# Stage a of a Fourier and maxout kernel as four 48x64 matmuls on quarters of the array, batches 3 to 7

## Chip, cores and metric

One core of one Trainium2 chip. The metric is the device time of one execution in microseconds (us). Times of the kernel before come from three runs and from one further execution that the hardware profiler recorded.

## What is computed

The input `x` has 8 batches of 3072 positions with 256 features. Each batch goes through a real Fourier transform along the positions, a complex 256x256 product with a bias, a soft threshold and the inverse transform. Every position then goes through three 256x768 products, whose elementwise maximum goes through a 768x256 product.

```
X = np.fft.rfft(x, axis=1)
Yr = Xr @ w_r - Xi @ w_i + b_r
Yi = Xr @ w_i + Xi @ w_r + b_i
Y = np.sign(Y) * np.maximum(np.abs(Y) - 0.01, 0.0)      # both parts
y = np.fft.irfft(Y, n=3072, axis=1)
h = np.maximum(np.maximum(y @ w1, y @ w2), y @ w3)
out = h @ w_out
```

## The kernel before

A position is written as n = 32*n1 + n2, with 96 values of n1 and 32 of n2. The forward transform has two steps. **Stage a** multiplies by a 96x96 table over n1: `load_x` (L460 on) brings four values of n2, a *quad*, as 96 rows of 1024 numbers (4 x 256 features); `split_x` makes two float16 halves of it, a high one on ACT and the remainder on DVE; `stage_a` multiplies the table, which is split likewise, by them and writes the result through `aq` to `a_d` in DRAM. Eight quads make a batch. **Stage b** (`load_a`, `split_a`, `stage_b`) reads `a_d` back in another layout and transforms over n2. `stage_w`, `stage_w2` and `finish_w` do the complex product and the threshold, `stage_q` begins the inverse transform and writes `z_d`, and `load_z`, `split_z` and `inverse` end it. `up` (three products and their maximum) and `down` do the rest.

A float32 product is made of three float16 ones, high by high, low by high and high by low: `mm3` issues them at L172, L173 and L174. So in stage a of batches 3 to 7 (the quads from `HALF_X` = 24 on, 40 in all) a quad is two groups of three matmuls, each with a 96x96 table as weights and 512 moving columns. The halves of that table (`f16`) lie in the tile `zeros`, whose name the profile shows. Batches 0 to 2 do stage a in float32 or in fp32r and are not touched.

The main loop runs over batches, over eight chunks of 384 positions, and over six slots (`f`) of a chunk. A slot is `up` for three weights (18 matmuls of 384 columns into three PSUM banks of the tag `up`) and `down` of an earlier slot (nine matmuls of 256 columns). All other stages of the next batch are put between the parts of the slots by a table of positions (`at`), measured in slots: a quad has position p = 5.6 slots per quad, loads at p - 8, `split_x` at p, `stage_a` at p + 1. `run_until` runs what is due, and a scheduler keeps each engine's instructions in the resulting order. The small operands come from the pools named in the code: `xq` has two buffers, the PSUM tiles `pa`, `px`, `py`, `pz` and `pi` share three banks (tag `ff`), and the tags `vl` and `vh` have three SBUF buffers each, used by batch 0 alone.

The lines that matter below: L172 to L174 (matmuls), L535 (ACT takes `pa` out of PSUM into `aq`), L539 (the ACT queue issues the store), L166 and L167 (the two halves of a split, on ACT and DVE), L905, L908 and L911 (ACT takes the first product of a slot out of PSUM, DVE the other two), L466 (load of a quad).

## Time and profile before

| | |
|---|---|
| median of 3 runs | 2024.7 us (2024.07 to 2025.35) |
| the profiled execution: its own time | 2026.48 us |
| its span, first to last instruction | 2024.7 us |
| TensorE (PE) busy | 2005.9 us, 99% |
| VectorE (DVE) busy | 1427.9 us, 71% |
| ScalarE (ACT) busy | 1046.7 us, 52% |
| granted TensorE clock | 0.999 of 2.4 GHz |

A matmul's duration in the profile counts from its start until its last result, and the next one starts earlier than that; what a matmul costs in a dense stream is the distance between two starts. PEld is the weight load, which the profile shows on a row of its own. An engine's idle time is put down to what released it.

### The profile page before, as it was taken

The page shows a single profiled execution, that of the slowest core. Times are in us where ns is not written, and L with a number is a line of the kernel's source. Part 1 is how long each engine was busy: PE and PEld are TensorE (multiplying, and loading weights), DVE is VectorE, ACT ScalarE, POOL GpSimd, SP SyncE. Part 2 cuts the span into 40 slices and gives each one's busy share as a digit, 9 for nine tenths or more (in the row PEclk, how much of TensorE's full clock was granted, in tenths as well). Part 3 has the DMA queues.
Part 4 walks back from the last instruction along what each step waited for, and adds up shares of the span by engine and source line. Part 5 has one row for each costly group of instructions (what it writes and reads, how often), then busy time and mean ns, then how long its engine had stood idle before and what let it go on. Part 6 is the DMA issues. An engine that isn't in the chain of part 4 may idle for free.

```text
span 2024.7 us, 40265 instructions
## 1 busy us (share of the span) xinstructions
PE 2005.9 (99%) x15822; PEld 1405.1 (69%) x15822; DVE 1427.9 (71%) x2726; ACT 1046.7 (52%) x2052; POOL 19.9 (1%) x75
## 2 busy tenths in 40 slices
PE   9999999999999999999999999999999999999999
PEld 5756766677776776767776777667777677776666
DVE  3787887687866877668776778757876577764454
ACT  4755654456545555455554565545554455543333
POOL 0000000000000000000000000000000000000000
PEclk9999999999999999999999999999999999999999
DMA  9645553454442453335442454333442333311110
GB/s 299 198 149 139 147 137 101 112 138 131 111 120 81 131 143 95 110 102 136 131 112 87 119 138 117 105 103 86 128 113 61 89 93 94 82 53 32 32 32 24
DMA packets 204560, 223.48 MB, mean 110 GB/s; under 512 B 20787, under 2 KB 179123, under 8 KB 204275
## 3 DMA queue, kind: packets, MB, share of 16 engines
q1 hardware_dynamic: 143603, 145.39, 27.6%
q10 hardware_dynamic: 59744, 72.11, 11.2%
q0 software_dynamic: 1024, 3.41, 0.5%
q8 instruction: 125, 2.05, 0.4%
q14 instruction: 64, 0.52, 0.1%
HBM read 103.13 MB, written 75.50 MB: 88 GB/s over the span
## 4 chain that ended last, share of the span: by engine, by line
PE 95%; DVE 2%; DMA 1%; ACT 1%; issue 1%; SPq 0%; ACTq 0%; DVEq 0%
PE pu L172 18%; PE pu L174 18%; PE pu L173 18%; PE pd L174 6%; PE pd L173 6%; PE pd L172 6%; PE py L174 3%; PE py L173 3%; PE py L172 3%; PE px L675 2%; PE pa L532 1%; PE pi L174 1%; PE pi L172 1%; PE pa L172 1%; PE pi L173 1%; PE pa L174 1%
## 5 line engine op out<-in xcount | busy, mean ns | idle before, releaser
L172 PE MATMUL pu<-yh,wuh 128*128 128x384 f16 x2304 | 751.8, 326 | 3.0 <-ACT c L905 1.0
L174 PE MATMUL pu<-yh,wul 128*128 128x384 f16 x2304 | 751.3, 326 | 0.0
L173 PE MATMUL pu<-yl,wuh 128*128 128x384 f16 x2304 | 751.3, 326 | 0.0
L166 ACT ACTIVATE hh<-h 128x384 f16<-128x384 f32 x384 | 200.3, 522 | 501.3 <-DVE h L911 497.8
L908 DVE TENSOR_TENSOR c<-pu,c 128x384 f32<-128x384 f32 x384 | 212.5, 553 | 257.5 <-PE pu L174 154.1
L174 PEld LDWEIGHTS <-wul 128*128 128x128 f16 x2304 | 225.4, 98 | 149.7 <-issue 0.7
L173 PE MATMUL pd<-wol,hh 128*128 128x256 f16 x1152 | 313.8, 273 | 0.0
L172 PE MATMUL pd<-woh,hh 128*128 128x256 f16 x1152 | 313.8, 273 | 0.0
L173 PEld LDWEIGHTS <-wuh 128*128 128x128 f16 x2304 | 225.7, 98 | 126.8 <-issue 4.9
L174 PE MATMUL pd<-woh,hh 128*128 128x256 f16 x1152 | 313.5, 273 | 0.0
L172 PEld LDWEIGHTS <-wuh 128*128 128x128 f16 x2304 | 225.5, 98 | 124.4 <-issue 3.2
L167 DVE SCALAR_TENSOR_TENSOR hh<-h,hh 128x384 f16<-128x384 f32 x384 | 213.5, 556 | 135.0 <-ACT hh L166 132.9
L905 ACT ACTIVATE c<-pu 128x384 f32<-128x384 f32 x384 | 187.0, 487 | 175.9 <-PE pu L174 155.1
L911 DVE TENSOR_TENSOR h<-pu,c 128x384 f32<-128x384 f32 x384 | 211.7, 551 | 50.2 <-PE pu L174 46.4
L172 PE MATMUL py<-wch,tt 128*128 128x256 f16 x504 | 137.4, 273 | 0.0
L174 PE MATMUL py<-wch,tt 128*128 128x256 f16 x504 | 137.3, 273 | 0.0
L173 PE MATMUL py<-wcl,tt 128*128 128x256 f16 x504 | 137.3, 272 | 0.0
L172 PEld LDWEIGHTS <-hh 128*128 128x128 f16 x1152 | 112.7, 98 | 33.7 <-issue 0.3
L173 PEld LDWEIGHTS <-hh 128*128 128x128 f16 x1152 | 112.7, 98 | 33.4
L940 ACT ACTIVATE o<-pd,s1u 128x256 f32<-128x256 f32 x191 | 82.8, 467 | 76.8 <-PE pd L174 35.4
L174 PEld LDWEIGHTS <-hh 128*128 128x128 f16 x1152 | 112.7, 98 | 13.8 <-DVE hh L167 0.5
L167 DVE SCALAR_TENSOR_TENSOR zl<-zq,s0u,zh 96x1024 f16<-96x1024 f32 (+1 forms) x72 | 82.7, 1157 | 4.4 <-ACT zh L166 4.3
(219 smaller groups left out, 2633.0 us busy)
## 6 DMA issues: line engine op xcount, KB each, us to landing
z_d<-zs ACTq DMA_DIRECT2D x96, 256.0 KB, 3.0
out_dram<-o ACTq DMA_DIRECT2D x190, 128.0 KB, 2.1
zq<-z_d SPq DMA_DIRECT2D x63, 384.0 KB, 4.0
ab<-a_d SPq DMA_DIRECT2D x84, 256.0 KB, 4.0
ab<-ab SPq DMA_DIRECT2D x336, 64.0 KB, 2.2
xq<-in_x_dram SPq DMA_DIRECT2D x55, 384.0 KB, 4.0
a_d<-aq ACTq DMA_DIRECT2D x53, 384.0 KB, 3.4
vb<-vb SPq DMA_DIRECT2D x308, 64.0 KB, 2.6
```

The source lines that it names most:

```text
L166: nc.scalar.activation(out=hi, in_=src, func=AF.Copy, scale=scale)
L167: later(lambda: low(nc.vector.scalar_tensor_tensor(out=lo, in0=src, scalar=scale, in1=h, op0=ALU.mult, op1=ALU.subtract)))
L172: nc.tensor.matmul(o, lh, rh, start=start, stop=False, **kw)
L173: nc.tensor.matmul(o, lh, rl, start=False, stop=False, **kw)
L174: st["mm"] = nc.tensor.matmul(o, ll, rh, start=False, stop=stop, **kw)
L532: nc.tensor.matmul(pa[0:96], fr, xp, start=True, stop=True)
L675: nc.tensor.matmul(pv[:, h, :, g // 2, g % 2], ah[:, g // 2, g % 2, h * P:(h + 1) * P], mb_sb[:, i, 4 * kb + g].rearrange("p (c m) -> p c ...
L905: st["act"] = nc.scalar.activation(out=c1, in_=p, func=AF.Copy)
L908: st["dve"] = nc.vector.tensor_tensor(out=c1, in0=p, in1=c1, op=ALU.max)
L911: st["dve"] = nc.vector.tensor_tensor(out=h32, in0=p, in1=st["c1"], op=ALU.max)
L940: nc.scalar.activation(out=o, in_=pd[t], func=AF.Copy, scale=st[b, "su"][1])
```

## The change

For n1 and n1 + 48 the table's rows are equal in the columns of even k1 and opposite in those of odd k1. So the change computes the 48 sums x[n1] + x[n1+48] and the 48 differences, and multiplies the sums by the 48 even columns and the differences by the 48 odd ones. The sums lie in partitions 0 to 47, the differences in 64 to 111. The tables are padded to 64 columns. Each product is cut into its two halves of 512 columns (`h`), and these go to PSUM partitions 0 to 63 and 64 to 127, so that four matmuls of 48 rows by 64 columns can lie on the four quarters of the array. A quad is then 12 matmuls of 512 columns, in three rounds of four, each with its own weight load, where there were six.

The operand takes four more loads and one cut in two: `xq` is loaded as rows 0 to 63 and, below them, again rows 0 to 47; a second pair of tiles (`x2`, in the buffers of `vl` and `vh`) gets the rows that lie 48 further on. A new step `sum_x`, one slot ahead of `split_x`, adds on DVE the second to the first with a sign per partition. The store becomes four.

```diff
+    even, odd = (np.pad(fa[0:48, np.arange(96) % 4 // 2 == i], ((0, 16), (0, 16))) for i in (1, 0))
+    tiled = np.block([[z, even], [z, odd]])
...
-    f16 = [zeros[0:N1, 128 * i:128 * i + 96] for i in range(2)]
+    ft = zeros[:, 384:512].rearrange("p (i m) -> p i m", i=2)
...
+    sign = small("sign")
+    nc.vector.memset(sign[0:64], 1.0)
+    nc.vector.memset(sign[64:P], -1.0)
...
-                xq = fft.tile([N1, NQ * D], F32, name="xq", bufs=2)
+                xq = fft.tile([P, NQ * D], F32, name="xq", bufs=2)
+                if q >= HALF_X:
+                    second = [
+                        fft.tile([P, 2, D], F32, name="x2", tag=tag, bufs=3) for tag in ("vl", "vh")
+                    ]
+                    xn = xq.rearrange("p (n d) -> p n d", n=NQ)
+                    for r, n in ((0, 64), (64, 48)):
+                        nc.sync.dma_start(out=xn[r:r + n], in_=xv[0:n])
+                    for i, t in enumerate(second):
+                        for r, n in ((0, 48), (48, 64)):
+                            nc.sync.dma_start(out=t[r:r + n], in_=xv[96 - n:96, 2 * i:2 * i + 2])
+                    st["x", q] = xq, second
+                    return
...
+    def sum_x(q):
+        xq, second = st.pop(("x", q))
+        with in_turn():
+            for i, t in enumerate(second):
+                half = xq[0:112, i * 512:i * 512 + 512]
+                nc.vector.scalar_tensor_tensor(
+                    out=half, in0=t[0:112].rearrange("p n d -> p (n d)"), scalar=sign[0:112], in1=half,
+                    op0=ALU.mult, op1=ALU.add,
+                )
+        st["x", q] = xq
...
     def split_x(q):
+        if q >= HALF_X:
+            xt = x_tile().bitcast(F16).rearrange("p i (h d) -> p i h d", h=2)[0:112]
+            for i in range(2):
+                with in_turn():
+                    split_later(
+                        xt[:, 0, i], xt[:, 1, i], pairs[0:112, i * 512:i * 512 + 512], st[b, "xx"][0:112]
+                    )
+            st["xs", q] = xt
+            return
...
     def stage_a(q):
+        if q >= HALF_X:
+            xt = st.pop(("xs", q))
+            pa = [ff_tile("pa") for _ in range(2)]
+            aq = fft.tile([P, NQ * D], F32, name="aq", bufs=2)
+            for t, i in ((0, 0), (0, 1), (1, 0)):
+                for r in range(2):
+                    rows = slice(64 * r, 64 * r + 48)
+                    for h in range(2):
+                        st["mm"] = nc.tensor.matmul(
+                            pa[r][64 * h:64 * h + 64], ft[rows, t], xt[rows, i, h],
+                            start=t == i, stop=t == 1,
+                        )
+            av = batch(b, "a").rearrange("(k e c) n d -> e k c (n d)", e=2, c=2)
+            for r in range(2):
+                o = aq[:, 512 * r:512 * r + 512]
+                nc.scalar.activation(out=o, in_=pa[r], func=AF.Copy, scale=1.0 / (X_SCALE * F_SCALE))
+                for h in range(2):
+                    n = q4 * NQ * D + h * 512
+                    nc.scalar.dma_start(out=av[1 - r, :, :, n:n + 512], in_=o[64 * h:64 * h + 48])
+            return
...
         at(p - (3 if b == 1 else 5 if b == 2 else 8), load_x, q)
+        if q >= HALF_X:
+            at(p - 1, sum_x, q)
         at(p, split_x, q)
         at(p + 1, stage_a, q)
```

Each engine's order shows where these stand. On PE, the last quad of batch 7 stood like this between two `up` products (`pa` is its PSUM bank, `xhl` the split operand, `zeros` the tile with the table):

```order
L174 MATMUL pu_20907<-yh_20754,wul_82 128x384
L172 LDWEIGHTS zeros_72
L172 MATMUL pa_20918<-xhl_20873,zeros_72 96x512
L173 LDWEIGHTS zeros_72
L173 MATMUL pa_20918<-xhl_20873,zeros_72 96x512
L174 LDWEIGHTS zeros_72
L174 MATMUL pa_20918<-xhl_20873,zeros_72 96x512
```

Now the same place has four matmuls, two to each of two banks, before the first bank is written again:

```order
L176 MATMUL pu_21583<-yh_21429,wul_82 128x384
L568 LDWEIGHTS zeros_72
L568 MATMUL pa_21593<-xhl_21550,zeros_72 64x512
L568 LDWEIGHTS zeros_72
L568 MATMUL pa_21593<-xhl_21550,zeros_72 64x512
L568 LDWEIGHTS zeros_72
L568 MATMUL pa_21594<-xhl_21550,zeros_72 64x512
L568 LDWEIGHTS zeros_72
L568 MATMUL pa_21594<-xhl_21550,zeros_72 64x512
L568 LDWEIGHTS zeros_72
L568 MATMUL pa_21593<-xhl_21550,zeros_72 64x512
```

Weight load and matmul still alternate, and the stage stands between the same neighbours.

On DVE, ahead of the same quad's split (`c1` and `h32` are the two results of `up` that DVE takes out of PSUM, `hh` and `yl` are remainders of splits), there stood:

```order
L911 TENSOR_TENSOR h32_20793<-pu_20786,c1_20751 128x384
L167 SCALAR_TENSOR_TENSOR hh_20795<-h32_20793,hh_20795 128x384
L167 SCALAR_TENSOR_TENSOR yl_20755<-pi_20806,yh_20754 128x384
L908 TENSOR_TENSOR c1_20827<-pu_20831,c1_20827 128x384
L911 TENSOR_TENSOR h32_20846<-pu_20839,c1_20827 128x384
L167 SCALAR_TENSOR_TENSOR hh_20848<-h32_20846,hh_20848 128x384
L908 TENSOR_TENSOR c1_20869<-pu_20877,c1_20869 128x384
L167 SCALAR_TENSOR_TENSOR xhl_20873<-xq_20336,xx_17743,xhl_20873 96x512
L167 SCALAR_TENSOR_TENSOR xhl_20875<-xq_20336,xx_17743,xhl_20875 96x512
```

and now:

```order
L965 TENSOR_TENSOR h32_21468<-pu_21461,c1_21426 128x384
L525 SCALAR_TENSOR_TENSOR xq_20994<-x2_20995,sign_91,xq_20994 112x512
L169 SCALAR_TENSOR_TENSOR hh_21470<-h32_21468,hh_21470 128x384
L525 SCALAR_TENSOR_TENSOR xq_20994<-x2_20996,sign_91,xq_20994 112x512
L169 SCALAR_TENSOR_TENSOR yl_21430<-pi_21481,yh_21429 128x384
L962 TENSOR_TENSOR c1_21502<-pu_21508,c1_21502 128x384
L965 TENSOR_TENSOR h32_21523<-pu_21516,c1_21502 128x384
L169 SCALAR_TENSOR_TENSOR hh_21525<-h32_21523,hh_21525 128x384
L962 TENSOR_TENSOR c1_21546<-pu_21553,c1_21546 128x384
L169 SCALAR_TENSOR_TENSOR xhl_21550<-xq_20994,xx_18299,xhl_21550 112x512 x2
```

The two sums come about one slot ahead of the split, with the remainder of `hh` and two PSUM results of `up` behind them.

On ACT the end of that quad was

```order
L905 ACTIVATE c1_20914<-pu_20907 128x384
L535 ACTIVATE aq_20917<-pa_20918 96x512
L535 ACTIVATE aq_20917<-pa_20923 96x512
L539 DMA a_d_18073<-aq_20917 96x1024
L820 ACTIVATE zs_20944<-pz_20937,s1v_14370 128x512
```

and is now

```order
L959 ACTIVATE c1_21590<-pu_21583 128x384
L575 ACTIVATE aq_21595<-pa_21593 128x512
L575 ACTIVATE aq_21595<-pa_21594 128x512
L578 DMA a_d_18641<-aq_21595 24x2x512 x4
L872 ACTIVATE zs_21629<-pz_21622,s1v_14790 128x512
```

Four stores stand where one stood; the rest is in the same order.

## Rows read from the trace of the kernel before

**Rows 1.** From the page: busy time of the engines, the granted clock in 40 slices (tenths), and the shares of the chain of work that ended last.

```profile
PE 2005.9 (99%) x15822; PEld 1405.1 (69%) x15822; DVE 1427.9 (71%) x2726; ACT 1046.7 (52%) x2052; POOL 19.9 (1%) x75
...
PEclk9999999999999999999999999999999999999999
...
PE 95%; DVE 2%; DMA 1%; ACT 1%; issue 1%; SPq 0%; ACTq 0%; DVEq 0%
```

**Rows 2.** Busy time by stretch; stage a of batches 3 to 7 runs from 382 to 1570 us. The columns are named in the first row.

```profile
core 0: us, PE busy (x) PEld busy (x) DVE busy (x) ACT busy (x) POOL busy (x), PEclk, DMA share, GB/s
...
380.00:680.00 300.00, 300.00 (x2468) 211.96 (x2467) 222.80 (x412) 161.83 (x321) 1.84 (x8) 1.00 0.43 116
680.00:980.00 300.00, 298.85 (x2448) 211.03 (x2446) 226.03 (x418) 161.97 (x321) 1.84 (x8) 1.00 0.44 120
980.00:1280.00 300.00, 300.00 (x2463) 212.09 (x2461) 224.78 (x416) 163.06 (x324) 1.84 (x8) 1.00 0.43 117
1280.00:1570.00 290.00, 289.63 (x2347) 204.00 (x2346) 204.58 (x386) 151.84 (x299) 3.68 (x16) 1.00 0.36 98
```

**Rows 3.** PE matmuls by line and shape over the whole run: count, busy us, mean ns of one, idle us of PE just before them and what ended it.

```profile
L172 PE MATMUL pu<-yh,wuh 128*128 128x384 f16 x2304 | 751.8, 326 | 3.0 <-ACT c L905 1.0 <-DVE c L908 1.0 <-ACT yh L166 0.4
...
L675 PE MATMUL px<-mb_all,ab 128*128 128x64 f16 x1344 | 53.0, 193 | 0.0
L172 PE MATMUL pa<-xhl,zeros 96*96 96x512 f16 x80 | 30.4, 380 | 0.0
L174 PE MATMUL pa<-xhl,zeros 96*96 96x512 f16 x80 | 30.3, 378 | 0.0
L173 PE MATMUL pa<-xhl,zeros 96*96 96x512 f16 x80 | 30.2, 378 | 0.0
L172 PE MATMUL pz<-vb,qh 128*128 128x512 f16 x77 | 29.2, 379 | 3.1 <-DMA vb<-vb 3.0
```

**Rows 4.** PE in order of time through the last quad of stage a: start us, duration us, line, operation.

```profile
1567.88 0.33 PE L174 MATMUL pu<-yh,wul 128*128 128x384 f16 x1
1568.04 0.38 PE L172 MATMUL pa<-xhl,zeros 96*96 96x512 f16 x1
1568.26 0.38 PE L173 MATMUL pa<-xhl,zeros 96*96 96x512 f16 x1
1568.47 0.38 PE L174 MATMUL pa<-xhl,zeros 96*96 96x512 f16 x1
1568.69 0.38 PE L172 MATMUL pa<-xhl,zeros 96*96 96x512 f16 x1
1568.90 0.38 PE L173 MATMUL pa<-xhl,zeros 96*96 96x512 f16 x1
1569.12 0.38 PE L174 MATMUL pa<-xhl,zeros 96*96 96x512 f16 x1
1569.34 0.33 PE L172 MATMUL pu<-yh,wuh 128*128 128x384 f16 x1
```

**Rows 5.** PE in order of time through one `stage_b`: the row of x16 is 16 matmuls of 64 columns, each with its own weight load.

```profile
1408.21 0.63 PE L675 MATMUL px<-mb_all,ab 128*128 128x64 f16 x16
1408.67 0.33 PE L172 MATMUL pu<-yh,wuh 128*128 128x384 f16 x1
```

**Rows 6.** Weight loads by line and shape over the whole run: count, busy us, mean ns of one.

```profile
L172 PEld LDWEIGHTS <-hh 128*128 128x128 f16 x1152 | 112.7, 98 | 33.7 <-issue 0.3
...
L172 PEld LDWEIGHTS <-zeros 96*96 96x96 f16 x80 | 9.8, 123 | 5.5
```

**Rows 7.** Weight loads in order of time in the last quad of stage a.

```profile
1567.88 0.12 PEld L172 LDWEIGHTS <-zeros 96*96 96x96 f16 x1
1568.04 0.12 PEld L173 LDWEIGHTS <-zeros 96*96 96x96 f16 x1
1568.26 0.12 PEld L174 LDWEIGHTS <-zeros 96*96 96x96 f16 x1
```

**Rows 8.** DVE instructions by line and shape over the whole run: count, busy us, mean ns of one, idle us before them.

```profile
L908 DVE TENSOR_TENSOR c<-pu,c 128x384 f32<-128x384 f32 x384 | 212.5, 553 | 257.5 <-PE pu L174 154.1 <-ACT c L905 96.5 <-ACT zh L166 5.0
...
L772 DVE SCALAR_TENSOR_TENSOR u<-py,s1x,cs 128x512 f32<-128x512 f32 x77 | 57.5, 747 | 25.0 <-PE py L174 20.8 <-ACT cs L762 4.2
...
L167 DVE SCALAR_TENSOR_TENSOR xhl<-xq,xx,xhl 96x512 f16<-96x512 f32 x80 | 56.8, 741 | 0.5
...
L581 DVE SCALAR_TENSOR_TENSOR ab<-ab 128x512 f16<-128x512 f32 x60 | 41.0, 683 | 4.8 <-ACT ab L578 4.0
```

**Rows 9.** DVE in order of time around the last quad: start us, duration us, line, operation, idle us before and what ended it.

```profile
1565.38 0.56 DVE L908 TENSOR_TENSOR c<-pu,c 128x384 f32<-128x384 f32 x1 [1.30 <-PE pu L174]
1565.85 1.40 DVE L167 SCALAR_TENSOR_TENSOR xhl<-xq,xx,xhl 96x512 f16<-96x512 f32 x2
1567.17 0.55 DVE L911 TENSOR_TENSOR h<-pu,c 128x384 f32<-128x384 f32 x1
1568.31 0.56 DVE L167 SCALAR_TENSOR_TENSOR hh<-h,hh 128x384 f16<-128x384 f32 x1 [0.59 <-ACT hh L166]
1570.58 0.56 DVE L908 TENSOR_TENSOR c<-pu,c 128x384 f32<-128x384 f32 x1 [1.71 <-PE pu L174]
```

**Rows 10.** ACT and its queue behind the same quad.

```profile
1568.89 1.24 ACT L535 ACTIVATE aq<-pa 96x512 f32<-96x512 f32 x2 [0.16 <-PE pa L174]
1570.16 0.33 ACTq L539 DMA_DIRECT2D a_d<-aq  x1
```

**Rows 11.** Waits of the SP queue: line, what it waited for, us in total, times, longest.

```profile
SPq L466 <- DVE xhl L167: 275.5, 25, 20.6
```

**Rows 12.** From the page: DMA issues, with count, KB each and median us from issue to landing.

```profile
xq<-in_x_dram SPq DMA_DIRECT2D x55, 384.0 KB, 4.0
a_d<-aq ACTq DMA_DIRECT2D x53, 384.0 KB, 3.4
vb<-vb SPq DMA_DIRECT2D x308, 64.0 KB, 2.6
```

More of the change, by code (lines that the diff above doesn't have):

```diff
@@ L88, in dft_tables @@
         halves(np.stack([np.concatenate([v, v]) for v in blocks], 1), SB),
-        np.ascontiguousarray(np.stack(mq + mb, 1)).astype(np.float32),
+        np.ascontiguousarray(np.stack(mq + mb + [tiled], 1)).astype(np.float32),
         np.eye(128, dtype=np.float32),
@@ L210, in quad_tile @@
     def quad_tile(name):
-        return fft.tile([96, NQ * D], F32, name=name, bufs=1 if name == "zq" else 2)
+        return fft.tile([P, NQ * D], F32, name=name, bufs=1 if name == "zq" else 2)[0:96]
     def s_tile(name):
@@ L240, in load_tables @@
         nc.sync.dma_start(out=id_sb, in_=ident)
+        st["tiled"] = s_tile("tiled")[:, 0:P]
+        nc.sync.dma_start(out=st["tiled"], in_=mq[:, 26])
     def load_last_bias():
@@ L464, in load_x @@
             else:
-                xq = fft.tile([N1, NQ * D], F32, name="xq", bufs=2)
+                xq = fft.tile([P, NQ * D], F32, name="xq", bufs=2)
[11 more added lines that the diff above has]
+                    return
+                xq = xq[0:N1]
             nc.sync.dma_start(out=xq.rearrange("p (n d) -> p n d", n=NQ), in_=xv)
@@ L502, in split_x @@
         pairs = st.pop(("x", q))
+        if q >= HALF_X:
[7 more added lines that the diff above has]
+            return
         parts = []
         for i, xp in enumerate(pairs):
-            if q >= HALF_X:
-                xt = x_tile().bitcast(F16)[0:N1]
-                xh, xl = xt[:, 0, 0:2 * D], xt[:, 1, 0:2 * D]
-                with in_turn():
-                    split_later(xh, xl, xp, st[b, "xx"][0:N1])
-                parts.append((xh, xl))
-                continue
             if q >= EARLY:
@@ L533, in stage_a @@
             else:
-                mm3(pa[0:96], *(f16 if q >= HALF_X else (fh, fl)), *xp)
+                mm3(pa[0:96], fh, fl, *xp)
             nc.scalar.activation(
-                out=aq[:, i * 512:i * 512 + 512], in_=pa[0:96], func=AF.Copy,
-                scale=1.0 / (X_SCALE * F_SCALE) if q >= HALF_X else 1.0,
+                out=aq[:, i * 512:i * 512 + 512], in_=pa[0:96], func=AF.Copy
             )
@@ L1019, in fourier_maxout_kernel @@
             if k == 0:
-                split_scaled(*f16, fr, F_SCALE)
+                split_scaled(ft[:, 0], ft[:, 1], st["tiled"][:, 64:P], F_SCALE)
             if k in (-2, 1, 4):
```

## Prediction

> **What bounds the kernel now.** I read the page first. PE is busy for 99% of the span, the chain of work that ended last lies on PE for 95%, and the granted clock is at its upper level, 2.4 GHz, in every slice [rows 1]; all prices below are at that level. Then the busy times by stretch: in the four stretches from 380 to 1570 us, where the changed stage runs, PE is idle for 1190.0 - 1188.5 = 1.5 us, while DVE is busy for 878 of 1190 us (74%) and ACT for 639 (54%) [rows 2]. So there a microsecond taken from the stream of matmuls is a microsecond of the kernel, and work on another engine costs nothing until it makes PE wait. The idle time by group says how little that happens: 3.0 us in front of 2304 matmuls of `up` and 3.1 us in front of `pz` [rows 3]. Last I read PE in order of time through one quad of stage a [rows 4].
>
> **What the change removes.** A matmul of the old stage lasts 0.38 us by its row [rows 3], but six of them start 0.216 us apart, and the next `up` starts 1569.34 - 1568.04 = 1.30 us after the first [rows 4]. That is the price in a dense stream. Forty quads (80 groups of three) hold 40 x 1.30 = 52.0 us.
>
> **What it puts there.** Twelve matmuls of 512 columns, each with a weight load. How long they take depends on how many are on the array at once, which no row of the trace before shows; I bound it. If none overlaps, a quad takes 12 x 0.216 = 2.59 us. If four overlap fully, 3 x 0.216 = 0.65 us. Between these, two smaller terms. Issue: in `stage_b` 16 pairs of weight load and matmul pass in 1408.67 - 1408.21 = 0.46 us, 0.029 us a pair [rows 5], so PE can hand out four pairs in 0.12 us, well inside the 0.216 us that one of them streams. Issue is then not the limit; it only staggers the four, and the last ends 3 x 0.029 = 0.09 us late: 0.65 + 0.09 = 0.74 us. I take the overlap as given, because the four matmuls of a round share nothing: two halves of the rows, two halves of the columns, two PSUM banks. Weight loads: one for 96 columns lasts 0.123 us against 0.098 us for 128 columns [rows 6], yet each starts with the matmul before it and is over long before that one is [rows 7], and the matmuls keep their 0.216 us. I expect the same of the 64-column ones.
>
> The second term is the passage between the whole array and its quarters, twice a quad. The lower end is nothing: from 128x128 to 96x96 weights and back PE shows ordinary distances, 0.16 and 0.22 us [rows 4]. The upper end is that each passage waits for the last results to leave, 0.38 - 0.216 = 0.163 us, and then exposes a weight load of 0.123 us: 2 x 0.286 = 0.57 us. I take one residue, 0.16 us, on the lower side of the middle, since the nearest row, the change of weight shape, costs nothing. A quad is then 0.74 + 0.16 = 0.90 us, and 40 x (1.30 - 0.90) = **16.0 us** go.
>
> The Trainium skill has a rule against this (TensorEngine Tiling (Array Packing), Tiling Modes, Key Properties): going from one tiling mode to another drains the engine. No run here shows a passage between modes. By that rule, paid in full at both ends, the sum would be about nothing instead of 16 us; it is the first rival.
>
> **What it adds elsewhere, each hidden.**
> - *DVE, two sums a quad.* The nearest rows are float32 operations of the same width, 0.683 us with a constant factor and 0.747 us with one per partition [rows 8]; I take 0.74. Eighty make 59 us, so DVE goes from 74% to 79% in that stretch. What could suffer is the release of PSUM banks. The product taken out at 1565.38 is done at 1565.94, and its bank is next written at 1569.34, three `up` products on [rows 4, 9]: 3.4 us to spare, against 1.48 us for both sums. DVE also stands idle for 154 us waiting for PE in front of L908 alone [rows 8]. If the slack were gone, the cost would be up to 40 x 1.48 = 59 us.
> - *DVE and ACT, the split.* The instructions keep their number and width (512 columns); 112 partitions instead of 96 change nothing that I charge. The sums stand a slot ahead of the split, some 5 us, and so do not delay it. The remainder of the second half is needed at the second matmul round instead of the fifth matmul; it is ready at 1567.25 and used from 1568.04 on [rows 4, 9].
> - *ACT, the store.* Four issues instead of one, 0.33 us each [rows 10]: 1 us more a quad, 40 us in all, on an engine that is half idle. Behind them stands the next `c` of `up`. Price if exposed: 40 us.
> - *PSUM.* Both `pa` banks are needed from the third matmul, 0.06 us in, not 0.65 us. There are three banks, and PE is not seen waiting for one here, so nothing is charged.
> - *SP, the loads.* Six issues of 896 KB in place of one of 384 KB: 40 x 512 KB = 20 MB more, 18 GB/s on the 98 to 120 GB/s of these stretches [rows 2]. The queue already stands still for a free `xq` for 275 us in 25 waits, up to 20.6 us each [rows 11]: loads are issued as early as a buffer allows and are needed far later than the 4.0 us that one takes to land [rows 12]. Five more issues hold the queue for perhaps 2 us a quad, an estimate from the 0.33 us of an issue on the other queue [rows 10] with some room. Behind them wait the moves of `vb`, 2.6 us to landing [rows 12], for which `pz` has waited 3.0 us in all [rows 3]. A late move could cost up to that 2 us in a few places; I charge nothing and keep it for the range.
> - *The start.* One 64 KB load and two small memsets before 50 us; nothing.
>
> **The sum.** The profiled execution took 2026.5 us, 1.8 us more than its span, which equals the median of the runs. 2026.5 - 16.0 = 2010.5 us for a profiled execution, 2008.7 us for a median run: **2009 us**. With both bounds of the switch and no other stall: 40 x (1.30 - 0.74) = 22 us less, 2002 us; with no stagger either, 26 us less, 1999 us; with 0.57 us of switching, nothing gained, 2025 us.
>
> **The rivals.**
> - *The passages eat the gain.* Each quad pays 0.34 to 0.6 us at its two ends: 1.08 to 1.34 us, so 2016 to 2026 us. For it: two passages a quad, 80 in all, for only three rounds of work between. Against it: the other changes of shape in rows 4 are free. Chance 0.17 (faster 0.07, same 0.06, slower 0.04).
> - *Slower: a weight load waits for the matmul on its own rows.* The place is inside a round. If the load for the right-hand quarter may not enter while the left-hand quarter of the same rows streams, the two column halves go one after the other and only the two row halves run side by side: six matmuls in turn per half. With the load behind the stream that is 6 x (0.216 + 0.029) = 1.47 us, 2024.7 + 40 x 0.17 = 2032 us; with the load behind the last result, 6 x (0.38 + 0.12) = 3.0 us and 2093 us. It decides from the point where a round takes over 1.30 / 3 = 0.43 us. Against it: on the whole array the load of the next weights starts with the matmul before it, on the same rows [rows 4, 7]. Chance 0.10. The Trainium skill states this rule (TensorE: Matmul & The Clock Gate, Part 3, what overlaps and what doesn't): weight loads overlap with running matmuls only where the row group differs. The trace disagrees for the whole array, at 1568.04; for quarters nothing here shows it.
> - *Nothing overlaps,* the change doesn't do what it says: 2.59 us a quad, 2024.7 + 40 x 1.29 = 2076 us. Nothing in the trace excludes it. Chance 0.06.
> - *A late engine.* The sums, the stores or the loads make PE wait. With 0.2 to 0.6 us a quad, 2017 to 2033 us; with both sums exposed, 2009 + 59 = 2068 us. Against it: the idle time of DVE and ACT in [rows 2, 9]. Chance 0.10 (faster 0.04, same 0.02, slower 0.04).
>
> **How the numbers follow.** About 0.2%, 4 us, is what a measurement can tell from no change. The forecast, quarters side by side with at most 0.34 us of switching, 1999 to 2016 us, has the rest, 0.57. Faster: 0.57 + 0.07 + 0.04 = 0.68. Same: 0.06 + 0.02 = 0.08. Slower: 0.04 + 0.10 + 0.06 + 0.04 = 0.24. The range runs from 2000 us, the full overlap, to 2035 us, past the first rival and the mild ends of the second and fourth. It leaves out the case of no overlap (0.06), most of the second rival (0.08), the far end of the fourth (0.03) and a hair below.
>
> **What would show it.** In the profile after, four starts of the new matmuls should lie within 0.1 us, rounds 0.22 us apart, and the next matmul of another kind should start about 0.90 us after the first; 0.74 means free passages, 1.3 that they eat the gain, and 1.47 or more that rounds do not hold together. DVE should be some 59 us busier with PE idle for no more than 3 us between 380 and 1570 us. The prediction is wrong in its main step if starts in a round lie 0.2 us apart, and in its cover if PE waits for DVE, ACT or a DMA there for over 5 us.

## The result, and the profile after

The change made the kernel slower: 2048.02 us, median of 4 runs (2047.35 to 2051.04), against 2025.03 us before (2024.07 to 2025.38). The ratio is 1.0117, interval 1.01 to 1.0135. The profiled execution took 2047.66 us, with a span of 2045.9 us, 21.2 us more than before. The forecast was 2009 us with a range up to 2035 us.

The first view is again the page: busy times, then the chain that ended last.

```profile
PE 2001.0 (98%) x16062; PEld 1384.5 (68%) x16062; DVE 1470.4 (72%) x2808; ACT 1036.0 (51%) x2052; POOL 22.4 (1%) x75
...
PE 48%; DVE 5%; DMA 4%; ACT 3%; issue 2%; ACTq 2%; SPq 0%; DVEq 0%
```

Beside [rows 1] the chain has changed its kind: PE's share has fallen from 95% to 48%, and the chain now runs through DVE, ACT, ACT's queue (ACTq) and transfers. (These shares add up to 64% only, where those before came near the whole span; so I read from this line which engines came onto the chain, and no sizes.) The clock is not the reason: it stands at its upper level in every slice, as before, 0.997 on average.

The second view is the busy time by stretch: from, to, length, then busy microseconds of PE, weight loads, DVE, ACT and POOL with their counts, granted clock, share of the DMA engines, GB/s.

```profile
380.00:680.00 300.00, 294.17 (x2501) 203.50 (x2500) 231.50 (x429) 155.86 (x314) 2.87 (x8) 1.00 0.48 132
680.00:980.00 300.00, 294.60 (x2499) 204.38 (x2498) 231.43 (x431) 158.61 (x321) 2.22 (x8) 1.00 0.49 135
980.00:1280.00 300.00, 291.15 (x2440) 200.51 (x2438) 229.99 (x429) 154.36 (x311) 2.21 (x8) 0.99 0.48 133
1280.00:1570.00 290.00, 281.26 (x2364) 194.39 (x2361) 211.00 (x397) 148.83 (x298) 4.43 (x16) 1.00 0.42 115
sum 1190.00, PE 1161.18 PEld 802.78 DVE 903.92 ACT 617.65 POOL 11.74; mean PE 290.29 PEld 200.70 DVE 225.98 ACT 154.41 POOL 2.93
```

PE is idle for 1190.0 - 1161.2 = 28.8 us where [rows 2] had 1.5 us. DVE is not full (904 of 1190 us), and ACT is *less* busy than before. Nothing here is an overloaded engine; something is late.

**Did the matmuls do what was forecast?** PE in order of time through the last quad of stage a, then the groups by form:

```profile
1588.96 0.33 PE L176 MATMUL pu<-yh,wul 128*128 128x384 f16 x1
1589.22 0.84 PE L568 MATMUL pa<-xhl,zeros 48*64 48x512 f16 x12
1589.99 0.34 PE L174 MATMUL pu<-yh,wuh 128*128 128x384 f16 x1
```

```profile
1589.21 0.36 PEld L568 LDWEIGHTS <-zeros 48*64 48x64 f16 x12 [0.32 <-issue]
```

```profile
L568 PE MATMUL pa<-xhl,zeros 48*64 48x512 f16 x480 | 33.7, 384 | 0.0
...
L525 DVE SCALAR_TENSOR_TENSOR xq<-x,sign,xq 112x512 f32<-112x512 f32 x80 | 57.8, 754 | 0.0
...
L174 PE MATMUL pu<-yh,wuh 128*128 128x384 f16 x2304 | 752.5, 327 | 14.2 <-ACT c L959 12.3 <-DVE c L962 1.0 <-DVE h L965 0.4
```

Yes. Twelve matmuls take 1589.99 - 1589.22 = 0.77 us where six took 1.30 us [rows 4]. Each matmul lasts 384 ns on its own, but 480 of them cover only 33.7 us: they overlap. The single records show starts at 0, 3, 6 and 10 ns, then 240 to 250 ns, then 456 to 466 ns: four at once, in three rounds. The sums cost DVE what was forecast (57.8 us) and never left it idle in front of them. What is new stands in the third row: 14.2 us of idle time in front of `up` [rows 3: 3.0 us], 12.3 us of it ended by ACT's `c`.

**Where the time went.** I take the stretch from the first matmul of the new stage to its last, and sum distances between starts of neighbouring matmuls, since busy times overlap and hide part of a wait. What a distance has above the ordinary one of its shape (0.16 us behind 384 columns, [rows 4]), if it is over 0.03 us, counts as PE waiting.

| in the stretch, us | before | after | difference |
|---|---|---|---|
| 40 quads of stage a, first start to next `up` | 51.9 | 31.0 | -20.9 |
| 40 distances ahead of the first `pa` | 5.7 | 9.4 | +3.7 |
| PE waiting elsewhere | 2.1 | 39.1 | +37.0 |
| stretch as a whole | 1186.5 | 1206.9 | +20.4 |

The three terms give +19.8 us of the +20.4. Ahead of the stretch and behind it nothing changed (382.6 and 382.8 us; 455.6 and 456.2 us). So the matmuls gave 17.2 us, and a new wait took 37.

**The new wait.** The list of waits: engine, line and what it waited for, us in total, times, longest. Then the issues of the store, as counts with shortest, median and longest duration in ns.

```profile
ACT zs L872 <- DMA a_d<-aq: 45.6, 14, 5.0
...
ACT c L959 <- DMA a_d<-aq: 29.1, 10, 3.4
ACT hh L168 <- DMA a_d<-aq: 28.8, 10, 3.5
...
PE pu L174 <- ACT c L959: 12.3, 15, 1.5
...
PE pd L174 <- ACT o L994: 4.9, 9, 0.9
```

```profile
L578 ACTq DMA_DIRECT2D a_d<-aq x160: 740/750/1517, 384.7 to 1593.2; - x160
```

ACT stands still for over 100 us under this heading, which the list of the kernel before does not have. Nearly all of it (95.6 of 103.5 us) stands right behind a store of `aq`. These are not waits for data to land: `zs` reads nothing of `aq`. The issues are made by ACT's own sequencer, and ACT's order in time shows what that means, first in an ordinary quad, then in the worst one:

```profile
1216.20 1.06 ACT L575 ACTIVATE aq<-pa 128x512 f32<-128x512 f32 x2
1216.81 3.24 ACTq L578 DMA_DIRECT2D a_d<-aq  x4
1220.10 0.69 ACT L872 ACTIVATE zs<-pz,s1v 128x512 f32<-128x512 f32 x1 [2.83 <-DMA a_d<-aq]
...
1246.61 1.06 ACT L575 ACTIVATE aq<-pa 128x512 f32<-128x512 f32 x2
1247.22 5.35 ACTq L578 DMA_DIRECT2D a_d<-aq  x4
1252.67 0.69 ACT L872 ACTIVATE zs<-pz,s1v 128x512 f32<-128x512 f32 x1 [5.00 <-DMA a_d<-aq]
1253.26 0.51 ACT L168 ACTIVATE hh<-h 128x384 f16<-128x384 f32 x1
...
1253.80 0.49 ACT L959 ACTIVATE c<-pu 128x384 f32<-128x384 f32 x1
...
1254.35 0.32 PE L174 MATMUL pu<-yh,wuh 128*128 128x384 f16 x1 [1.45 <-ACT c L959]
```

Four issues follow each other for 3.24 us, and ACT begins nothing else meanwhile. An issue takes 0.75 us, not the 0.33 us of [rows 10]. Behind them stand `zs`, `hh` and `c`, and PE stands 1.45 us at 1254.35 for the bank that `c` takes out. At 1247 even more came together: the chain of waits shows the third issue held until a store of the output had landed.

```profile
1244.44 6.53 DMA out_dram<-o
1250.97 0.02 issue
1250.99 0.02 ACTq L578
1251.01 0.04 issue
1251.05 0.74 ACTq L578
```

In 9 of the 40 quads the four issues took over 3.5 us. In five of these an issue began late, behind a wait like this one, in four a single issue itself lasted 1.1 to 1.5 us. All quads together took 9.0 us above 3.25 us a quad.

### The profile page after: what moved, and what is told of

It is laid out like the page before. It is cut to its first block, busy times and chain, and to the rows that moved or that the text cites. A ratio compares the mean times of both kernels' runs of the same rounds, so it can differ in the third digit from the quotient of the medians.

```text
span 2045.9 us, 41175 instructions
## 1 busy us (share of the span) xinstructions
PE 2001.0 (98%) x16062; PEld 1384.5 (68%) x16062; DVE 1470.4 (72%) x2808; ACT 1036.0 (51%) x2052; POOL 22.4 (1%) x75
## 4 chain that ended last, share of the span: by engine, by line
PE 48%; DVE 5%; DMA 4%; ACT 3%; issue 2%; ACTq 2%; SPq 0%; DVEq 0%
PE pu L174 10%; PE pu L176 10%; PE pu L175 10%; PE pd L174 3%; PE pd L176 3%; PE pd L175 3%; DMA a_d<-aq 2%; PE py L174 1%; PE py L176 1%; PE py L175 1%; ACTq L578 1%; PE px L727 1%; ACT aq L575 1%; DVE h L965 1%; ACT hh L168 1%
## 5 line engine op out<-in xcount | busy, mean ns | idle before, releaser
L174 PE MATMUL pu<-yh,wuh 128*128 128x384 f16 x2304 | 752.5, 327 | 14.2 <-ACT c L959 12.3
L872 ACT ACTIVATE zs<-pz,s1v 128x512 f32<-128x512 f32 x84 | 57.2, 681 | 80.1 <-DMA a_d<-aq 45.6
```

The lines of the kernel that those rows point to most:

```text
L174: nc.tensor.matmul(o, lh, rh, start=start, stop=False, **kw)
L872: st["zs"] = nc.scalar.activation(out=zs, in_=pv, func=AF.Copy, scale=st[b, "sv"][1] if b else -1.0)
```

## The experiments

The theory was that the four issues, made by ACT, keep ACT away too long. "Absence" below is the mean time from PE's going on after the stage until the last issue is out: 1.83 us before, 4.96 us in the change. "PE waiting" is the sum of the table above. Rivals were the sums on DVE, the larger loads, the place of the evictions, and the shape of the transfers. Absence and waiting come from the one profiled execution of each run. Each ratio is against the kernel before on the same chip, median 2024.9 to 2027.1 us. e3, e4, e6 and e13 put the rows of `a_d` in other places, e5 leaves out the sums and e8 the second loads.

| run | edit to | median us | ratio, interval | absence | PE waiting |
|---|---|---|---|---|---|
| before | | 2025.03 | 1 | 1.83 | 2.1 |
| the change | | 2048.02 | 1.0117, 1.01 to 1.0135 | 4.96 | 39.1 |
| e1_store_sp | change | 2016.12 | 0.9952, 0.9937 to 0.9967 | | 6.9 |
| e2_store_pool | change | 2010.04 | 0.992, 0.9905 to 0.9934 | | 2.9 |
| e3_one_store | change | 2011.78 | 0.9931, 0.9914 to 0.9947 | 2.23 | 4.5 |
| e4_before_four | before | 2038.38 | 1.0059, 1.0044 to 1.0074 | 4.24 | 14.2 |
| e5_no_sums | change | 2043.97 | 1.0089, 1.0072 to 1.0106 | 4.84 | 36.3 |
| e6_flat_four | change | 2026.24 | 1.0, 0.9991 to 1.001 | 3.92 | 19.4 |
| e7_half_pool | change | 2015.62 | 0.9956, 0.9941 to 0.9972 | 3.19 | 9.9 |
| e8_no_second | change | 2044.39 | 1.0099, 1.0084 to 1.0114 | 4.89 | 35.3 |
| e9_dve_evac | change | 2043.57 | 1.0092, 1.0074 to 1.011 | 4.81 | 34.7 |
| e10_before_pool | before | 2024.27 | 0.9998, 0.9988 to 1.0008 | | 0.2 |
| e11_split_hold | change | 2020.58 | 0.9979, 0.9969 to 0.9989 | two parts | 12.4 |
| e12_pad | change | 2060.96 | 1.0164, 1.0144 to 1.0184 | | 29.0 |
| e13_before_late | before | 2041.96 | 1.0066, 1.0048 to 1.0085 | 4.42 | 16.5 |

### Who makes the issues: e1, e2 and e10

```diff
-                    nc.scalar.dma_start(out=av[1 - r, :, :, n:n + 512], in_=o[64 * h:64 * h + 48])
+                    nc.sync.dma_start(out=av[1 - r, :, :, n:n + 512], in_=o[64 * h:64 * h + 48])   # e1
+                    nc.gpsimd.dma_start(out=av[1 - r, :, :, n:n + 512], in_=o[64 * h:64 * h + 48]) # e2
```

e1, from SP's queue:

> The changed kernel with the four stores of a quad issued by the SP queue instead of ACT's; nothing else differs. Theory S (stores): in the trace of the change the four stores hold ACT's queue for 3.2 us a quad (0.74 to 0.80 us each, against one of 0.33 us before), ACT comes late to what stands behind them, and PE waits: 39 us of waiting, against 18 us that the matmuls gave. Without them on ACT the wait should fall to some 5 us: 2005 to 2016 us, ACT's wait behind a_d gone. Theory V (the two sums on DVE hold up the releases of PSUM): no change, 2044 to 2052 us. Theory L (20 MB more loads and more transfers under way make landings late): no change or worse, 2044 to 2060 us, since SP has more to issue.

e2, from POOL's queue:

> The changed kernel with the four stores of a quad issued by the POOL queue, which is otherwise idle for 99% of the time. Theory S: ACT and SP are both free of them, 2003 to 2014 us, at best the whole gain of the matmuls, 2024.7 - 18 = 2007 us. Theory V: no change, 2044 to 2052 us. Theory L: no change, 2040 to 2052 us.

With nothing altered but the queue, the time falls by 32 us (e1) and 38 us (e2). e1 lies on the edge of what was expected, since 4 us more of waiting than in e2 remain (five waits for `c`; why they remain is not shown). e2 is faster than the kernel before, by 0.8% (interval 0.66 to 0.95%), and is the best version found. Its stretch lasts 1170.3 us, 16.2 us less than before, which is the forecast of the prediction for the matmuls. The sum of the four stretches, then POOL and ACT in order of time, and the first of PE's waits:

```profile
sum 1190.00, PE 1188.13 PEld 827.72 DVE 936.84 ACT 636.04 POOL 105.73; mean PE 297.03 PEld 206.93 DVE 234.21 ACT 159.01 POOL 26.43
```

```profile
1254.18 0.59 POOL L578 DMA_DIRECT2D a_d<-aq  x1 [28.00 <-ACT aq L575]
1257.57 1.76 POOL L578 DMA_DIRECT2D a_d<-aq  x3 [2.80 <-issue]
```

```profile
1253.29 1.09 ACT L575 ACTIVATE aq<-pa 128x512 f32<-128x512 f32 x2 [1.06 <-PE pz L176]
1254.26 0.50 ACT L959 ACTIVATE c<-pu 128x384 f32<-128x384 f32 x1
```

```profile
PE pu L174 <- ACT c L959: 2.8, 7, 0.7
```

PE is idle for 1.9 us of the 1190. Right behind the two evictions ACT goes on with `c` at 1254.26. In this quad, the slowest, POOL has the last issue out over 5 us after the first began; the median quad takes 2.3 us. On average the last is out 4.21 us behind PE's going on, as late as ACT's in e4, and nobody waits for it: the lateness of a store by itself costs nothing here.

e10 does the same to the kernel before, so that a gain of the queue by itself would show:

```diff
-        (nc.scalar if b else nc.gpsimd).dma_start(
+        (nc.scalar if b and q < HALF_X else nc.gpsimd).dma_start(
```

> The kernel before with its one store a quad, batches 3 to 7, on the POOL queue: a control for the version of the change with stores on POOL, which took 2010 us. If that version's gain comes from the matmuls, this is the kernel before within 3 us, 2022 to 2028 us, since PE waited for 2 us in the stretch and one issue took 0.33 us of ACT. If moving stores off ACT is itself worth something here: 2008 to 2018 us.

2024.27 us, no difference (0.9998, 0.9988 to 1.0008). The gain of e2 is that of the matmuls.

### How many issues, and of what shape: e3, e4 and e6

e3 makes one store a quad, 96 rows of 4 KB, on ACT. e4 gives the kernel before the four stores of the change. e6 keeps four stores, each to 48 neighbouring rows.

```diff
 e3
-                for h in range(2):
-                    n = q4 * NQ * D + h * 512
-                    nc.scalar.dma_start(out=av[1 - r, :, :, n:n + 512], in_=o[64 * h:64 * h + 48])
+            nc.scalar.dma_start(out=batch(b, "a")[:, q4 * NQ:(q4 + 1) * NQ, :],
+                                in_=aq[0:96].rearrange("p (n d) -> p n d", n=NQ))
 e4 (in the kernel before)
+        if q >= HALF_X:
+            av = batch(b, "a").rearrange("(k e c) n d -> e k c (n d)", e=2, c=2)
+            for r in range(2):
+                for h in range(2):
+                    n = q4 * NQ * D + h * 512
+                    nc.scalar.dma_start(out=av[1 - r, :, :, n:n + 512],
+                                        in_=aq[48 * h:48 * h + 48, 512 * r:512 * r + 512])
+            return
 e6
-            av = batch(b, "a").rearrange("(k e c) n d -> e k c (n d)", e=2, c=2)
+            av = batch(b, "a").rearrange("(e k) n d -> e k (n d)", e=2)
-                    nc.scalar.dma_start(out=av[1 - r, :, :, n:n + 512], in_=o[64 * h:64 * h + 48])
+                    nc.scalar.dma_start(out=av[1 - r, :, n:n + 512], in_=o[64 * h:64 * h + 48])
```

> The changed kernel with one store of 96 rows by 1024 on ACT's queue, as before the change, in place of the four; the rows then land in the wrong places of a_d (this part of the computation is changed). Theory S: the price is the number and shape of the issues, not their queue: 0.33 us on ACT, PE waits for about 5 us, 2004 to 2012 us. Theory V: 2044 to 2052 us. Theory L: 2040 to 2050 us, three transfers of twelve fewer.

> The kernel before with only the stores of the change: in batches 3 to 7 four stores of 48 rows by 512 with the change's pattern in DRAM, on ACT's queue, in place of one (the rows land in the wrong places of a_d: this part of the computation is changed). Theory S: the stores alone cost what PE lost, about 39 us: 2045 to 2075 us, with ACT's queue held for some 3.2 us a quad. Theory V and theory L: within 5 us of the kernel before, 2020 to 2030 us, since sums and loads are absent.

> The changed kernel with its four stores on ACT's queue, but each goes to 48 neighbouring rows of a_d instead of 24 pairs of rows four apart (one level of rows in DRAM instead of two; the rows land in the wrong places: this part of the computation is changed). If the price of an issue hangs on its shape: 0.33 us each as the one store before, 1.3 us of hold a quad, PE waits for under 10 us: 2005 to 2018 us. If four issues cost what four issues cost: 0.74 to 0.80 us each, 2044 to 2052 us.

One store brings the gain back (2011.78 us) with the work on the array unchanged. Four stores alone slow the kernel before by 12 us: the right direction, less than the 20 us and more that were expected. So four stores are enough to do harm without any of the new matmuls, but not all of the harm. e6 fell between its two ranges: issues become cheaper, 0.43 us in the median, and the time falls to 2026.24 us, a little over half of the way to e3. ACT in order of time there, and the issues:

```profile
1208.26 1.90 ACTq L578 DMA_DIRECT2D a_d<-aq  x4
```

```profile
L578 ACTq DMA_DIRECT2D a_d<-aq x160: 308/433/3007, 386.3 to 1573.8; - x160
```

Four such issues take 1.90 us where nothing holds them; single ones take up to 3.0 us. The shape of the target (24 x 2 rows apart, or 48 neighbouring ones) thus moves the price of an issue, and four of them still cost more than the one of e3.

### Neither the sums nor the loads: e5 and e8

```diff
 e5: sum_x without its two instructions
...
-            for i, t in enumerate(second):
-                half = xq[0:112, i * 512:i * 512 + 512]
-                nc.vector.scalar_tensor_tensor(out=half, in0=t[0:112]...
 e8: no second loads, the sums read xq twice
-                    second = [fft.tile([P, 2, D], F32, name="x2", tag=tag, bufs=3) for tag in ("vl", "vh")]
+                    second = [None, None]
...
-                            nc.sync.dma_start(out=t[r:r + n], in_=xv[96 - n:96, 2 * i:2 * i + 2])
...
-                    out=half, in0=t[0:112].rearrange("p n d -> p (n d)"), scalar=sign[0:112], in1=half,
+                    out=half, in0=half, scalar=sign[0:112], in1=half,
```

> The changed kernel, its four stores on ACT's queue as in the change, without the 80 sums on DVE: x2 is still loaded but not added (this part of the computation is left out). Four stores alone made PE wait for 14 us in the kernel before, in the change PE waits for 39 us; open is where the other 25 come from. Theory SV (the stores hold ACT and the sums take the slack that DVE had to make up for it): the wait falls to some 14 us, 2016 to 2026 us. Theory SL (the extra loads do): 2040 to 2050 us, no change. Theory SP (the shorter stage itself, which fills two PSUM banks at once and frees them only after ACT): no change, 2040 to 2050 us.

> The changed kernel, four stores on ACT's queue, without the four loads of x2 a quad; the sums stand and read xq twice (this part of the computation is left out). Theory SL: the wait falls from 39 to some 14 us, 2016 to 2026 us. Theory SV and theory SP: no change, 2040 to 2050 us.

2043.97 and 2044.39 us: each alone is worth at most some 4 us of the 23, little more than the scatter of the runs, and PE still waits for 36.3 and 35.3 us. As main causes both fell.

### Absence in a row: e7, e9 and e11

e7 gives two of the four stores to POOL, e9 lets DVE take out the second bank, and e11 makes the two stores of the second bank one slot later.

```diff
 e7
-                    nc.scalar.dma_start(...
+                    (nc.scalar if h else nc.gpsimd).dma_start(...
 e9
-                nc.scalar.activation(out=o, in_=pa[r], func=AF.Copy, scale=1.0 / (X_SCALE * F_SCALE))
+                if r:
+                    nc.vector.tensor_scalar(
+                        out=o, in0=pa[r], scalar1=1.0 / (X_SCALE * F_SCALE), scalar2=None, op0=ALU.mult)
+                else:
+                    nc.scalar.activation(out=o, in_=pa[r], func=AF.Copy, scale=1.0 / (X_SCALE * F_SCALE))
 e11: store(q, aq, r) holds the two dma_start of one bank
+                if r == 0:
+                    store(q, aq, r)
...
+    def store_rest(q):
+        store(q, st.pop(("aq", q)), 1)
...
+            at(p + 2, store_rest, q)
```

> The changed kernel with two of the four stores on the POOL queue and two on ACT's: ACT is held for some 1.6 us a quad instead of 3.2. If the wait grows in proportion to the hold (none at 0.3 us, 39 us at 3.2 us): some 17 us of waiting, 2020 to 2028 us. If PE has a slack of about two microseconds that is used up first: 2 to 8 us of waiting, 2007 to 2015 us. Theories V and L: 2044 to 2052 us.

> The changed kernel, four stores on ACT's queue as in the change, but DVE takes the second of the two pa banks out of PSUM. From the traces so far, the time from PE going on after stage a until ACT is free for other work is 1.8 us on average before the change, 2.0 us with stores off ACT, 3.3 us with two of them, 4.3 us in the kernel before with four, 5.0 us in the change; PE's waiting in the stretch is 2, 3 to 7, 10, 14 and 39 us. Neither the sums nor the loads removed the difference between the last two. Theory A (it is ACT's absence alone: the change begins both evictions after its short stage, the kernel before one of them during its long stage): taking one eviction of 0.59 us from ACT brings the absence to some 4.4 us and the waiting to 12 to 20 us: 2017 to 2030 us. Theory B (the two banks held together, or the sheer number of transfers, cost the rest): the waiting stays over 30 us, 2038 to 2052 us; DVE's extra 0.6 us a quad makes it rather worse.

> The changed kernel with all four stores still on ACT's queue, but the two of the difference half one slot later than the two of the sum half: the same number of issues and of transfers, the same time of ACT in all, in two pieces of some 1.6 us. In the traces so far PE's waiting follows the time from PE going on after stage a until the last of the issues that stand in a row is out: 1.8 us and 2 us of waiting before the change, 3.2 us and 10 us with two stores on ACT, 4.2 us and 14 us in the kernel before with four, 4.8 to 5.0 us and 35 to 39 us in the change and in the three trials that kept its four stores together. Theory H (one long absence of ACT in a row is what costs): the first piece ends some 3.3 us after PE goes on, 5 to 15 us of waiting, 2009 to 2020 us. Theory N (the number of issues and transfers, or ACT's time in all): no change, 2040 to 2050 us.

e7: 2015.62 us, between its two ranges; the absence falls to 3.19 us and the waiting to 9.9 us. e9 came out at 2043.57 us, in the range of its theory B: it took an eviction of 0.5 us from ACT, but the absence hardly changed (4.81 us), and neither did the time. The first issue begins 1.48 us behind PE's going on, where it was 1.50 us in the change. The rows show one such quad: `vb` stands where the second eviction stood, and the four issues still stand in one run. Of what theory B names, e11 speaks against the number of transfers, e13 against the two banks.

```profile
1185.98 0.57 ACT L580 ACTIVATE aq<-pa 128x512 f32<-128x512 f32 x1
1186.46 0.71 ACT L168 ACTIVATE vb<-u,s0v 128x512 f16<-128x512 f32 x1
1186.58 3.23 ACTq L583 DMA_DIRECT2D a_d<-aq  x4
```

e11 is the cleanest: the same issues, the same number, the same engine, only in two runs.

```profile
1231.28 1.62 ACTq L564 DMA_DIRECT2D a_d<-aq  x2
...
1235.15 1.53 ACTq L564 DMA_DIRECT2D a_d<-aq  x2
```

It takes 2020.58 us, 27 us less than the change, a hair above its range. ACT's time in issues (124 us in the stretch, 125 in the change) was not the price; 3.2 us of it *in a row* was. Sorted by absence, the runs with the new stage wait longer at each step: 2.2 us, 4.5 us of waiting; 3.2, 10; 3.9, 19; 4.8 to 5.0, 35 to 39. Those with the old stage lie lower: 1.8, 2; 4.2 to 4.4, 14 to 17. So the absence counts, but it is not all. The prediction had a number of this size: a product's bank is next written three `up` products on, with 3.4 us to spare [rows 4, 9]. For the bank that ACT empties the trace before gives the same: 3.88 us in the median from the end of a product to the next write of its bank, less 0.49 us for `c`. It is no sharp bound, for at 3.2 us of absence PE waits already.

### What is left between e4 and the change: e12 and e13

With four stores the kernel before waits for 14.2 us, the change for 39.1 us. e12 puts three idle matmuls of 384 columns in front of the first `up` behind each stage (in 30 of 40 quads right behind it), so that the two together last about as long as the old stage. e13 goes the other way: it lets the kernel before, with its four stores, take both banks out only after the stage, as the change does.

```diff
 e12
+            st["pad"] = 3
...
+        for _ in range(st.pop("pad", 0)):
+            nc.tensor.matmul(p, wuh[:, i, 0, f * P:(f + 1) * P], y[0][:, 0], start=True, stop=True)
 e13 (e4, and)
+            xs, pas = st.pop(("xs", q)), [ff_tile("pa") for _ in range(2)]
+            for n, (t, j) in enumerate(((0, 0), (0, 1), (1, 0))):
+                for i in range(2):
+                    st["mm"] = nc.tensor.matmul(pas[i][0:96], f16[t], xs[i][j], start=n == 0, stop=n == 2)
+            for i in range(2):
+                nc.scalar.activation(out=aq[:, i * 512:i * 512 + 512], in_=pas[i][0:96], ...
```

> The changed kernel with three idle matmuls of 384 columns behind each stage a (the first matmul of the next up product, issued three times more): 40 x 3 x 0.163 = 19.5 us more of matmuls, about what the quarters saved (20.9 us). Open is why four stores cost 14 us of waiting in the kernel before and 39 us in the change. Theory P (behind a quad ACT sets the pace for a while, so that what PE saves in the stage turns into waiting; PE's added work fills it): the time hardly changes, 2042 to 2054 us, and the waiting falls to some 15 to 25 us. Theory R (the rest comes from something else of the change that is still there: its transfers, its two banks): the matmuls are added in full, 2062 to 2070 us, with 35 us of waiting or more.

> The kernel before with the four stores of the change (rows land in the wrong places of a_d: this part of the computation is changed) and, beyond that, its six matmuls of a quad in another order: the two banks in turn, so that both end with the stage and ACT begins both evictions only then, as in the change. The stage keeps its 1.30 us. In the kernel before with four stores alone PE waited for 14 us, in the change for 39 us, and filling the stage's saving with idle matmuls took 10 us of that away. Theory E (the late start of the first eviction is the rest): the absence of ACT behind the stage grows from 4.2 to some 4.8 us and the waiting to 25 to 35 us: 2048 to 2062 us. Theory R (something else of the change): 10 to 18 us of waiting, 2034 to 2043 us.

e12 came between its two ranges: 19.5 us of matmuls lengthened the stretch by 9.0 us only, to 1215.9 us, and the waiting fell by 10.1 us, to 29.0 us. So about 10 us of the change's waiting is its own shorter stage: while ACT is away, a faster PE merely arrives earlier at the same late bank. e13, in the range of its theory R, adds 2 us of waiting to e4 (16.5 us): the late eviction is a small part. Of the 25 us between e4 and the change this settles about 12, if the two add up. By what ended the waits, the change has 14.6 us for `c`, 7.0 us for `o` (ACT's eviction behind `down`), 6.6 us for a remainder on DVE that follows on ACT and 4.2 us for a move of `vb`; e4 has 2.8, 3.0, 2.6 and 3.9 us. So most of the difference is still waiting for ACT. But e12 and e13 differ by 12.5 us at nearly the same length of the stage and nearly the same absence (4.59 us in e12, counted from behind the idle matmuls where these follow the stage at once, and 4.42 us in e13), so the mean absence does not explain it. The sums and the loads can hold some 3 to 4 us each at most (e5, e8); whether these add up was not tried. The longer runs of issues are another candidate: 9.0 us above 3.25 us a quad in the change, 2.1 us in e4; but in e9 they fall to 3.9 us and the waiting falls only to 34.7 us. **Of some 13 us the cause is not shown.**

## Why the prediction was wrong, step by step

- *The bound.* Right: PE's stream was the bound, and e2 shows that a microsecond taken from it is one of the kernel, when no other engine comes late.
- *The removal, 52.0 us.* Right: 51.9 us by all 40 quads.
- *The new matmuls and the passages, 0.90 us a quad.* Right: 0.77 us and 0.09 us more ahead of the first `pa`, 0.87 us. The stagger was smaller than taken (3 ns a start, not 29), rounds are 0.23 us apart. The 29 ns of [rows 5] were no price of an issue: going by the 0.216 us of 512 columns, 64 columns stream in some 27 ns (an estimate), so that row shows the streaming. 17.2 us went, 16.0 were forecast. The first three rivals fell with this. On the second, the Trainium skill (TensorE: Matmul & The Clock Gate, Part 3, what overlaps and what doesn't) lets a weight load overlap with a running matmul only in another row group; the trace disagrees for quarters too: all twelve loads are over 0.36 us after the first began, while the rounds, which use the same rows three times, run for 0.77 us. On the first, the Trainium skill (TensorEngine Tiling (Array Packing), Tiling Modes, Key Properties) has the engine drain between tiling modes; with all that a quad has above three rounds, this costs here no more than 0.87 - 0.65 = 0.22 us.
- *DVE, SP, PSUM, start: hidden.* Right: DVE's sums and SP's loads within some 4 us each (e5, e8). PE was never idle in front of the new matmuls, and ahead of the stretch nothing changed; PSUM and the start were not tried alone.
- *ACT, the store: "four issues instead of one, 0.33 us each", "on an engine that is half idle", 1 us more a quad.* **This is the step that failed, twice.** The size: an issue of the new shape took 0.75 us, so 3.24 us a quad instead of 1.3. The duration had been taken from the same line of code with another shape (96 rows of 4 KB, against 24 x 2 rows of 2 KB). The trace before had a warning in the same queue, which I had not read; issues of the output store, ns:

```profile
L941 ACTq DMA_DIRECT2D out_dram<-o x190: 546/548/1245, 149.0 to 2020.9; - x190
```

Of two shapes on one queue one took 0.33 us and one 0.55 us; the shape counts, and for a third shape the range should have reached above 0.55 us. The cover, which weighs more: "half idle" is an average over 1190 us. What mattered was how long ACT may be away *in a row*, and the 3.4 us computed for DVE's bank, a few lines above in the prediction, were never held against ACT's. With 3.24 us of issues behind the evictions ACT was away for 3.96 us or more in every quad, and PE waited over 0.1 us within 10 us behind 25 of the 40. The right size alone would not have saved it: with 1.3 us, as charged, the absence would be some 2.23 + 3 x 0.33 = 3.2 us, an estimate from e3 and [rows 10], and e7 with 3.19 us still waited for 9.9 us.
- *The rival that came.* "A late engine" was on the list, with 0.2 to 0.6 us a quad; it came to 37 / 40 = 0.93 us. The text itself named the price of this one: 40 us if exposed, behind it "the next `c` of `up`". 2009 + 40 = 2049 us would have been the time. That it fits is luck: the 40 us were the time of the added issues at 0.33 us, while ACT in fact spent 125 us in issues instead of 13, and 37 us of that reached PE. The case was left out of the range, which ended at the mild ends of the rivals.

The test stated at its end worked: PE waiting for ACT for over 5 us was to show that the cover was wrong, and in front of `up` alone it waited for `c` for 12.3 us.

## What to carry to other kernels

An issue of a DMA is an instruction of the engine that makes it: count issues in a row on an in-order engine, price each by a row of the same shape, and where there is none let the range reach above the dearest issue in the trace; then hold the sum against the slack of the next instruction there, not against the engine's idle share. When a change cuts one transfer into several, look first for a queue whose engine nobody waits for. And when the predicted gain is there in the matmuls but not in the time, sum start distances over the stretch: the gain and the new wait come apart, and one line (e2) puts the store elsewhere and keeps the gain, 2010.04 us.

## What the runs showed of the hardware

- Four matmuls on quarters of the array, 48 rows and 64 columns each, started 3 ns apart and ran side by side; a quad of twelve took 0.77 us and some 0.1 us more at its entry.
- The price of an issue of the same 96 KB: 0.75 us from ACT and 0.77 us from SP (medians; 24 x 2 rows of 2 KB), 0.43 us from ACT to 48 neighbouring rows, and 0.59 us from POOL (24 x 2 rows again). For the old store, 96 rows of 4 KB, it was 0.33 us from ACT and 0.51 us from POOL (e10). The Trainium skill calls the SP and ACT path generally faster than POOL's (DMA: Bandwidth & Descriptors, Issuing engine by pattern); for the time of an issue, which is what cost here, that held for the old store, and for the new one POOL was the fastest of the three.
- An issue can also wait for an older transfer: at 1250.97 us of the change the third store left only when a store of the output had landed, 6.53 us after that one was issued. In e6 single issues took up to 3.0 us; what held these is not shown.
